# One exponential per attention slot from PSUM, with the sum taken beside it, and earlier strided loads in a fused attention and expert kernel

## The chip, the cores and the metric

The kernel runs on one core of a Trainium2 chip. The metric is the device time of one execution in microseconds, the median of several runs. TensorE (PE) multiplies, VectorE (DVE) and ScalarE (ACT) work elementwise and read PSUM, GpSimd (POOL) only builds masks at the start, and SyncE (SP) issues nearly all the transfers.

## The reference

All is float32. Attention of 2 batches, 8 heads, 576 positions of 64 numbers; the first four heads use a local mask of 32 positions, the last four a strided one (equal position modulo 32). Three products and a sum over four experts follow, on 1152 tokens.

```
scores = where(mask, q @ k.T / 8, -1e9)
scores = scores - max(scores)
attn   = exp(scores);  attn = attn / (sum(attn) + 1e-9)
x      = attn @ v                      # (1152, 512)
x      = ((x @ w1) * (x @ w2)) @ w3 @ w_out
out    = sum over 4 experts of p[:, e] * (relu(x @ e1[e]) @ e2[e])
```

## The kernel before

Every product after attention is made of three, from a high and a low part of each operand (`mm3`). The wide weights w1, w2, w_out and w3 arrive as 64-bit numbers and are turned into float32 and split on ACT and DVE: for each `Chunk` of 1 MB, ACT rounds the low word (L136) and takes the magnitude (L144), DVE clamps, shifts, sets the sign and adds (L147 to L157), ACT makes the high part `w_hi` (L164) and DVE the low part `w_lo` (L174). The generator `work` gives these steps out one at a time; `advance` and `need` drive it. `add` ends a chunk's use of its raw buffer and issues the load of a later one on SP's queue (`load_next`), so a raw load waits there for DVE.

Attention of a batch is cut into six chunks (`Chunk4`), three local ones with six slots of 64 columns and three strided ones with eight slots of 54. A slot is one row of scores for each of the 128 partitions, and all slots of a chunk lie in one bank of PSUM. `attend(b, s)` writes out step s of nine: scores of chunk s+1 on PE, maxima and exponentials of chunk s, sums and normalisation of chunk s-1, transposes of chunk s-2 with their copy out of PSUM by ACT (L375), and values of chunk s-3 with the two halves of the result, x_hi on ACT (L423) and x_lo on DVE (L427). The order of instructions on each engine is the order of the code (a manual schedule), and each engine works its queue in that order. PSUM has three banks for scores and five (`bank`) that products, transposes and values take in turn.

The nine steps of the first batch stand before all products; only dummy matmuls (`keep_warm`) lie between them on PE. The nine steps of the second batch stand between the 32 units of the first product (`run_unit`, two sums of 12 matmuls each, `ab_acc`); each unit ends in a copy on ACT (L462) and a multiplication on DVE (L464). Unit 2i and 2i+1 of a batch need chunk i of w1 and w2, called c0 to c7 below.

The loads of the second batch's strided heads, keys and queries (`load_qk(1, 1)`) and values (`load_v_str(1)`), are issued in the main loop:

```
            run_unit()
            if done == 1:
                load_qk(1, 1)
                load_v_str(1)
```

Of the kernel before, what the change touches and what calls it, by code (L numbers as in the profile page):

```python
# [8 lines left out]
F32 = mybir.dt.float32  # L9
# [4 lines left out]
AF = mybir.ActivationFunctionType  # L14
ALU = mybir.AluOpType
# [3 lines left out]
P = 128  # L19
# [13 lines left out]
SCALE = 1.0 / float(D) ** 0.5  # L33
# [9 lines left out]
def kernel(  # L43
# [13 lines left out]
    nc = tc.nc  # L57
# [8 lines left out]
    small = ctx.enter_context(tc.tile_pool(name="small", bufs=4))  # L66
# [122 lines left out]
    loaded = 0  # L189
# [47 lines left out]
    def advance(n=1):  # L237

        return all([next(worker, False) for _ in range(n)])
# [14 lines left out]
    qk, vals = {}, {}  # L254

    def load_qk(b, g, cut=0):

        tq, tk = (big[b].tile([P, 2, S], F32, tag="big", name=name) for name in ("tq", "tk"))
        pairs = slice(2 * g, 2 * g + 2)
        for c in ([slice(0, cut), slice(cut, S)] if cut else [slice(0, S)]):  # L260
            for t, src, queue in ((tk, kT, nc.sync), (tq, qT, nc.scalar if cut else nc.sync)):
                queue.dma_start(out=t[:, :, c], in_=src[b, pairs, :, c].rearrange("k p n -> p k n"))
        qk[b, g] = (tq, tk)

    def load_v_loc(b, c):

        tv = wp.tile([P, 2, 3, P], F32, tag="w", name="tv_loc")

        def load(dst, rows, t0, n):
            nc.sync.dma_start(out=dst, in_=v_loc[b, :, rows, t0:t0 + n].rearrange("k p t d -> p k t d"))  # L270

        lower, upper, middle = slice(0, 64), slice(64, P), slice(W, 3 * W)
        if c == 0:
            load(tv[lower, :, 0:1], lower, 0, 1)
            load(tv[upper, :, 0:1], middle, 0, 1)
            load(tv[:, :, 1:], slice(0, P), 1, 2)
        elif c == 1:
            load(tv, slice(0, P), 3, 3)
        else:
            load(tv[lower, :, 0:1], lower, 0, 1)  # L280
            load(tv[upper], middle, 3, 3)
            load(tv[lower, :, 1:], middle, 1, 2)
        vals[b, 0, c] = tv

    def load_v_str(b):

        threes = [wp.tile([P, n, P], F32, tag="w", name="tv_str") for n in (8, 4)]
        for tv, t0, n in ((threes[0], 0, 4), (threes[1], 4, 1)):
            for k in range(2):
                nc.sync.dma_start(out=tv[64 * k:64 * k + T3, :2 * n].rearrange("p (h t) d -> p h t d", h=2),  # L290
                                in_=v_str[b, k, :2 * T3, t0:t0 + n].rearrange("(h p) t d -> p h t d", h=2))
        for k in range(2):
            nc.sync.dma_start(out=threes[1][64 * k:64 * k + NB, 2:], in_=v_str[b, k, 2 * T3:2 * T3 + NB, :2])
        vals[b, 1] = threes

    class Chunk4:
# [44 lines left out]

        def maxima(self):
            s = self.slots
            mx = small.tile([P, 8], F32, tag="mx", name="mx")
            nc.vector.tensor_reduce(out=mx[:, :s], in_=self.sc, axis=mybir.AxisListType.X, op=ALU.max)
            self.frame = p_ring[self.index % 4]
            self.p = self.frame[:, :s, :self.nk]
            nc.vector.tensor_tensor(out=self.p, in0=self.sc, in1=self.wide(mx), op=ALU.subtract)

        def wide(self, t):  # L350
            return t[:, :self.slots].unsqueeze(2).to_broadcast([P, self.slots, self.nk])

        def exps(self):
            nc.scalar.activation(self.p, self.p, AF.Exp, scale=SCALE)

        def sums(self):
            s = self.slots
            self.rec = small.tile([P, 8], F32, tag="rec", name="rec")
            rec = self.rec[:, :s]
            nc.vector.tensor_reduce(out=rec, in_=self.p, axis=mybir.AxisListType.X, op=ALU.add)  # L360
            nc.vector.tensor_scalar_add(rec, rec, 1e-9)
            nc.vector.reciprocal(rec, rec)

# [176 lines left out]
    class Weights:  # L540
# [17 lines left out]
        def work(self):  # L558
# [20 lines left out]
            if self.again:  # L579
                for i, u in enumerate(sums):  # L580
                    nc.sync.dma_start(out=u.bitcast(F32), in_=stored[self.at][i])
            else:
                yield from self.split(sums, w)
                for i, u in enumerate(sums):
                    nc.sync.dma_start(out=stored[self.at][i], in_=u.bitcast(F32))
# [121 lines left out]
    with tc.manual_schedule():  # L707
# [17 lines left out]
        load_qk(1, 0)  # L725
        for c in range(3):
            load_v_loc(1, c)
        chunks = [[Chunk4(3 * g + c, b, g, c) for g in range(2) for c in range(3)] for b in range(B)]
        units = [(b, ft, i) for b in range(B) for ft in range(8) for i in range(2)]
        done = 0  # L730
# [3 lines left out]
        def run_unit():  # L734

            nonlocal done, rest
            b, ft, i = units[done]
            need(c_w12[ft])
            block = ab_block(b, ft, i)
            for _ in range(2):  # L740
                next(rest, None)
                next(block)
                advance(1)
            rest = block
            done += 1
            if b == i == 1:
                c_w12[ft].free()

        def attend(b, s):

            nonlocal live
            chunk = chunks[b]
            n = len(chunk)
            if s == 0:
                chunk[0].scores()
            if s + 1 < n:
                chunk[s + 1].scores()
            if s < n:
                chunk[s].maxima()
                chunk[s].exps()  # L760
            if 1 <= s <= n:
                chunk[s - 1].sums()
                chunk[s - 1].normalise()
            if 2 <= s < n + 2:
                chunk[s - 2].transposes()
                chunk[s - 2].evac(nc.scalar.copy)
            if 3 <= s:
                c = chunk[s - 3]
                c.pv()
                c.put()  # L770
                c.put_lo()
                if c.g == 0 or c.c > 0:
                    live -= 1

        for s in range(9):
            attend(0, s)
            keep_warm(8 if s < 8 else 20)
            if s > 3:
                advance(2)
        steps = iter(range(9))  # L780
        while done < 16:
            run_unit()
            if done == 1:
                load_qk(1, 1)
                load_v_str(1)
            if done in (2, 4, 5, 7, 8, 10, 11, 13, 14):
                attend(1, next(steps))
        load_probs()
# [161 lines left out]
```

## Time and profile before

| what | before |
|---|---|
| median of 3 runs | 644.78 us (644.19 to 645.07) |
| the profiled execution | 647.61 us, of which 645.9 us span |
| PE busy | 626.6 us, 97% of the span, 4688 matmuls |
| DVE busy | 454.8 us, 70% |
| ACT busy | 265.0 us, 41% |
| mean granted clock of TensorE | 0.986 of full speed |

The span runs from the first instruction to the last. PE is busy nearly throughout, but its dummy matmuls count as busy too, so the first 35 us can't be read from its share. A granted clock of 1.00 is 2.4 GHz, of 0.50 it is 1.2 GHz.

### The profile page before, as it was taken

To read this page: it belongs to the slowest core of one execution; us is meant where nothing else is said; L and a number is where in the kernel's file an instruction comes from. 1 tells how busy PE (TensorE), PEld (TensorE's weight loads), DVE (VectorE), ACT (ScalarE), POOL (GpSimd) and SP (SyncE) were. 2 spreads that over 40 slices of the span, in tenths; PEclk is the share of its full clock that TensorE was granted. 3 is DMA by queue.
4 is the path that set the end of the run, shared out by engine and by line. 5 is a ranking of instruction groups with operands and counts; after the bars stand their busy time and mean duration, and the time that the engine had idled before them with its cause. 6 is when DMAs were issued, how large, how long until landed. Compare 5 with 4: busy or idle time off the path is not lost.

```text
span 645.9 us, 11412 instructions
## 1 busy us (share of the span) xinstructions
PE 626.6 (97%) x4688; PEld 569.9 (88%) x4688; DVE 454.8 (70%) x825; ACT 265.0 (41%) x455; POOL 4.2 (1%) x19
## 2 busy tenths in 40 slices
PE   9898998999998999999999999999999999999997
PEld 6687888999886999998999889988788989999996
DVE  5887995698875423777787787797776576665843
ACT  3653563566555322433333333344433333333321
POOL 2000000000000000000000000000000000000000
PEclk9799997999998999999999999999999999999999
DMA  8864322144433310234444355434478464656311
GB/s 263 283 235 128 132 71 76 66 142 136 168 132 130 128 54 15 66 131 159 168 156 171 131 196 163 162 131 152 173 248 323 164 246 154 226 183 236 130 66 66
DMA packets 28727, 99.45 MB, mean 154 GB/s; under 512 B 2652, under 2 KB 6740, under 8 KB 26116
## 3 DMA queue, kind: packets, MB, share of 16 engines
q1 hardware_dynamic: 28132, 98.14, 43.5%
q8 instruction: 37, 0.61, 0.4%
q10 hardware_dynamic: 544, 0.59, 0.3%
q14 instruction: 14, 0.11, 0.0%
HBM read 79.58 MB, written 19.14 MB: 153 GB/s over the span
## 4 chain that ended last, share of the span: by engine, by line
PE 71%; DVE 11%; DMA 9%; ACT 5%; issue 3%; SPq 1%; DVEq 0%; ACTq 0%
PE g_acc L247 10%; PE g_acc L248 10%; PE g_acc L249 10%; DMA raw<-in_w3T_dram 4%; PE m_a L247 4%; PE m_a L249 4%; PE m_a L248 4%; PE x_acc L247 3%; PE x_acc L248 3%; PE x_acc L249 3%; PE m_b L249 3%; PE m_c L247 3%; PE m_b L248 3%; PE m_c L248 3%; PE m_c L249 3%
## 5 line engine op out<-in xcount | busy, mean ns | idle before, releaser
L616 ACT ACTIVATE h_hi<-u 128x320 fp32r<-128x320 f32 (+1 forms) x128 | 56.9, 445 | 188.9 <-DVE u L622 188.9
L247 PE MATMUL g_acc<-w_hi,h_hi 128*128 128x512 f32 (+1 forms) x296 | 114.3, 386 | 0.0
L248 PE MATMUL g_acc<-w_lo,h_hi 128*128 128x512 f32 (+1 forms) x296 | 114.2, 386 | 0.0
L249 PE MATMUL g_acc<-w_hi,h_lo 128*128 128x512 f32 (+1 forms) x296 | 113.7, 384 | 0.0
L247 PE MATMUL ab_acc<-x_hi,w_hi 128*128 128x288 f32 x256 | 77.9, 304 | 2.5 <-ACT w_hi L164 1.6
L622 DVE TENSOR_TENSOR u<-m_b,u 128x320 f32<-128x320 f32 (+1 forms) x96 | 40.8, 452 | 53.2 <-PE m_b L249 53.2
L555 DVE TENSOR_TENSOR w_lo<-raw,w_hi 128x768 fp32r<-128x768 f32 x64 | 69.4, 1084 | 12.0 <-ACT w_hi L553 11.9
L249 PE MATMUL ab_acc<-x_hi,w_lo 128*128 128x288 f32 x256 | 76.7, 300 | 0.8 <-DVE w_lo L174 0.8
L248 PE MATMUL ab_acc<-x_lo,w_hi 128*128 128x288 f32 x256 | 76.6, 299 | 0.7 <-DVE x_lo L427 0.7
L249 PEld LDWEIGHTS g_acc<-w_hi,h_lo 128*128 128x128 f32 x296 | 55.6, 188 | 11.6
L247 PEld LDWEIGHTS g_acc<-w_hi,h_hi 128*128 128x128 f32 x296 | 55.8, 188 | 8.0
L248 PEld LDWEIGHTS g_acc<-w_lo,h_hi 128*128 128x128 f32 x296 | 55.7, 188 | 7.6
L618 DVE SCALAR_TENSOR_TENSOR h_lo<-u,h_hi 128x320 fp32r<-128x320 f32 (+1 forms) x128 | 57.6, 450 | 3.5 <-ACT h_hi L616 1.1
L553 ACT CAST w_hi<-raw 128x768 fp32r<-128x768 f32 x64 | 59.9, 936 | 0.0
L247 PEld LDWEIGHTS ab_acc<-x_hi,w_hi 128*128 128x128 f32 x256 | 49.2, 192 | 3.8 <-ACT w_hi L164 1.7
L249 PEld LDWEIGHTS ab_acc<-x_hi,w_lo 128*128 128x128 f32 x256 | 49.1, 192 | 1.2 <-DVE w_lo L174 1.2
L248 PEld LDWEIGHTS ab_acc<-x_lo,w_hi 128*128 128x128 f32 x256 | 49.1, 192 | 0.9 <-DVE x_lo L427 0.9
L248 PE MATMUL m_b<-b_t,s_hi 128*128 128x320 f32 (+1 forms) x128 | 37.9, 296 | 0.0
L622 DVE TENSOR_TENSOR u<-m_a,u 128x320 f32<-128x320 f32 (+1 forms) x64 | 28.8, 450 | 11.6 <-PE m_a L249 11.6
L555 DVE TENSOR_TENSOR s_lo<-raw,s_hi 128x1024 fp32r<-128x1024 f32 x16 | 19.6, 1225 | 23.2 <-ACT s_hi L553 23.2
L136 ACT ACTIVATE raw<-raw 128x1024 int32<-128x1024 uint32 x20 | 23.4, 1168 | 28.4 <-DMA raw<-in_w3T_dram 19.2
L622 DVE TENSOR_TENSOR u<-m_c,u 128x320 f32<-128x320 f32 (+1 forms) x64 | 29.0, 452 | 4.8 <-PE m_c L249 4.2
(151 smaller groups left out, 1392.8 us busy)
## 6 DMA issues: line engine op xcount, KB each, us to landing
raw<-in_e_dram SPq DMA_DIRECT2D x32, 1024.0 KB
raw<-in_w_dram SPq DMA_DIRECT2D x8, 1024.0 KB
raw<-in_w3T_dram SPq DMA_DIRECT2D x8, 1024.0 KB
stored<-s_hi SPq DMA_DIRECT2D x16, 512.0 KB
stored<-s_lo SPq DMA_DIRECT2D x16, 512.0 KB
s_hi<-stored SPq DMA_DIRECT2D x16, 512.0 KB
s_lo<-stored SPq DMA_DIRECT2D x16, 512.0 KB
raw<-in_w_out_dram SPq DMA_DIRECT2D x4, 1024.0 KB
```

The source lines that it names most:

```text
L136: nc.scalar.activation(self.low, self.low.bitcast(U32), AF.Copy, scale=2.0 ** -29)
L247: mm(acc, lh, rh, start=first, stop=False)
L248: mm(acc, lh, rl, start=False, stop=False)
L249: mm(acc, ll, rh, start=False, stop=last)
L553: nc.scalar.copy(dst[0], src)
L555: nc.vector.tensor_tensor(out=dst[1], in0=src, in1=dst[0].bitcast(F32), op=ALU.subtract)
L616: nc.scalar.activation(hi, src, AF.Relu)
L618: nc.vector.scalar_tensor_tensor(out=lo, in0=src, scalar=0.0, in1=hi.bitcast(F32), op0=ALU.max, op1=ALU.subtract)
L622: nc.vector.tensor_tensor(out=out, in0=acc, in1=b, op=ALU.add)
```

## The change

The maximum is multiplied by -SCALE after the reduction (a tiny instruction on DVE), and then each slot has its own ACT instruction that reads the scores from PSUM, takes the slot's maximum as bias and adds its results up into `rec`. The subtraction over the whole chunk (L348) and the sum over the whole chunk (L360) leave DVE. The two loads move: keys and queries go ahead of the main loop, right behind the second batch's local values, and the strided values to the moment when the third raw chunk has been issued.

```diff
         def maxima(self):
             s = self.slots
-            mx = small.tile([P, 8], F32, tag="mx", name="mx")
-            nc.vector.tensor_reduce(out=mx[:, :s], in_=self.sc, axis=mybir.AxisListType.X, op=ALU.max)
+            self.mx = small.tile([P, 8], F32, tag="mx", name="mx")
+            mx = self.mx[:, :s]
+            nc.vector.tensor_reduce(out=mx, in_=self.sc, axis=mybir.AxisListType.X, op=ALU.max)
+            nc.vector.tensor_scalar_mul(mx, mx, -SCALE)
             self.frame = p_ring[self.index % 4]
             self.p = self.frame[:, :s, :self.nk]
-            nc.vector.tensor_tensor(out=self.p, in0=self.sc, in1=self.wide(mx), op=ALU.subtract)
...
         def exps(self):
-            nc.scalar.activation(self.p, self.p, AF.Exp, scale=SCALE)
+            self.rec = small.tile([P, 8], F32, tag="rec", name="rec")
+            for s in range(self.slots):
+                at = slice(s, s + 1)
+                nc.scalar.activation(self.p[:, s], self.sc[:, s], AF.Exp, bias=self.mx[:, at], scale=SCALE,
+                                     accum_out=self.rec[:, at])
 
         def sums(self):
-            s = self.slots
-            self.rec = small.tile([P, 8], F32, tag="rec", name="rec")
-            rec = self.rec[:, :s]
-            nc.vector.tensor_reduce(out=rec, in_=self.p, axis=mybir.AxisListType.X, op=ALU.add)
+            rec = self.rec[:, :self.slots]
             nc.vector.tensor_scalar_add(rec, rec, 1e-9)
             nc.vector.reciprocal(rec, rec)
...
         load_qk(1, 0)
         for c in range(3):
             load_v_loc(1, c)
+        load_qk(1, 1)
...
             if s > 3:
                 advance(2)
+            if loaded == 3 and (1, 1) not in vals:
+                load_v_str(1)
         steps = iter(range(9))
         while done < 16:
             run_unit()
-            if done == 1:
-                load_qk(1, 1)
-                load_v_str(1)
             if done in (2, 4, 5, 7, 8, 10, 11, 13, 14):
```

ACT's queue in steps 4 and 5 of the first batch before (`p_pair` holds the probabilities, `sc` the scores, `mx` the maxima, `tp` the transposes, `o` the values' products, `raw_212` chunk c0's raw words):

```order
L354 ACTIVATE p_pair<-p_pair 128x8x54
L375 COPY pT<-tp 128x384
L423 CAST x_hi<-o 128x2x3x32 x2
L136 ACTIVATE raw_212<-raw_212 128x1024
L354 ACTIVATE p_pair<-p_pair 128x8x54
L375 COPY pT<-tp 128x512
```

The same place in ACT's queue now:

```order
L358 ACTIVATE p_pair,rec<-sc,mx 128x54 x8
L377 COPY pT<-tp 128x384
L425 CAST x_hi<-o 128x2x3x32 x2
L136 ACTIVATE raw_212<-raw_212 128x1024
L358 ACTIVATE p_pair,rec<-sc,mx 128x54 x8
L377 COPY pT<-tp 128x512
```

Nothing changed places; each exponential of a chunk became eight instructions (six for a local chunk) ahead of the same copy and the same x_hi.

DVE's queue in step 4 of the first batch before (maxima of chunk 4, sums and normalisation of chunk 3, x_lo of chunk 1):

```order
L345 TENSOR_REDUCE mx<-sc 128x8
L348 TENSOR_TENSOR p_pair<-sc,mx 128x8x54
L360 TENSOR_REDUCE rec<-p_pair 128x8
L361 TENSOR_SCALAR rec<-rec 128x8
L362 RECIPROCAL rec<-rec 128x8
L365 TENSOR_TENSOR p_pair<-p_pair,rec 128x8x54
L427 TENSOR_TENSOR x_lo<-o,x_hi 128x2x3x32 x2
```

The same step now:

```order
L346 TENSOR_REDUCE mx<-sc 128x8
L347 TENSOR_SCALAR mx<-mx 128x8
L363 TENSOR_SCALAR rec<-rec 128x8
L364 RECIPROCAL rec<-rec 128x8
L367 TENSOR_TENSOR p_pair<-p_pair,rec 128x8x54
L429 TENSOR_TENSOR x_lo<-o,x_hi 128x2x3x32 x2
```

Two long instructions are gone and a tiny one has come; x_lo still stands at the end of the step, ahead of the next step's maxima.

SP's queue of transfers behind the second batch's local values, as a difference (`raw` numbers differ between the builds; the rows taken out are the loads of c2 and c3, the row put in is c2's):

```order
 L270 DMA tv_loc<-in_v_loc_dram 64x2x384
 L270 DMA tv_loc<-in_v_loc_dram 64x2x256
-L132 DMA raw_635<-in_w_dram 128x2048
-L132 DMA raw_733<-in_w_dram 128x2048
 L262 DMA tk<-in_kT_dram 128x2x576
 L262 DMA tq<-in_qT_dram 128x2x576
+L132 DMA raw_669<-in_w_dram 128x2048
 L290 DMA tv_str<-in_v_str_dram 54x2x512 x2
 L290 DMA tv_str<-in_v_str_dram 54x2x128 x2
 L293 DMA tv_str<-in_v_str_dram 18x256 x2
```

Keys and queries now go ahead of c2's load, the strided values between c2's and c3's; before, all of them stood behind c3's load and ahead of c4's.

## Rows read from the trace of the kernel before

**Rows 1.** Busy time by stage: start and end, length, each engine's busy us (instructions), granted clock, DMA
```profile
0.00:34.70 34.70, 30.88 (x605) 23.62 (x606) 25.54 (x57) 15.72 (x34) 4.24 (x19) 0.90 0.86 280
...
60.00:80.00 20.00, 18.86 (x272) 17.48 (x271) 18.68 (x36) 10.88 (x20) 0.00 (x0) 1.00 0.31 107
...
140.00:646.00 506.00, 498.01 (x2984) 453.02 (x2982) 344.92 (x623) 194.00 (x326) 0.00 (x0) 1.00 0.43 153
```

**Rows 2.** Timeline of PE, 34 to 104 us: start, length, instruction, idle time before and its releaser
```profile
36.57 0.40 PE L248 MATMUL ab_acc<-x_lo,w_hi 128*128 128x288 f32 x1 [0.69 <-DVE x_lo L427]
...
58.95 0.52 PE L370 MATMUL tp<-ident,p_pair 128*128 128x128 f32 x3 [2.58 <-DVE p_pair L365]
...
73.48 0.52 PE L370 MATMUL tp<-ident,p_pair 128*128 128x128 f32 x3 [0.78 <-DVE p_pair L365]
...
78.56 0.40 PE L247 MATMUL ab_acc<-x_hi,w_hi 128*128 128x288 f32 x1 [0.37 <-ACT pT L375]
...
87.43 0.63 PE L370 MATMUL tp<-ident,p_pair 128*128 128x128 f32 x4 [0.78 <-DVE p_pair L365]
...
102.01 0.43 PE L247 MATMUL ab_acc<-x_hi,w_hi 128*128 128x288 f32 x1 [1.61 <-ACT w_hi L164]
```

**Rows 3.** Timeline of DVE in the first batch
```profile
17.16 0.61 DVE L348 TENSOR_TENSOR p_pair<-sc,mx 128x432 f32<-128x432 f32 x1
17.68 0.59 DVE L360 TENSOR_REDUCE rec<-p_pair 128x8 f32<-128x432 f32 x1
18.31 0.17 DVE L361 TENSOR_SCALAR rec<-rec 128x8 f32<-128x8 f32 x1
...
23.92 0.61 DVE L427 TENSOR_TENSOR x_lo<-o,x_hi 128x192 fp32r<-128x192 f32 x2
...
36.06 0.85 DVE L427 TENSOR_TENSOR x_lo<-o,x_hi 128x108 fp32r<-128x108 f32 x4
```

**Rows 4.** Timeline of ACT in the first batch
```profile
7.72 0.52 ACT L354 ACTIVATE p_pair<-p_pair 128x384 f32<-128x384 f32 x1 [5.49 <-DVE p_pair L348]
...
14.13 0.57 ACT L354 ACTIVATE p_pair<-p_pair 128x432 f32<-128x432 f32 x1 [1.32 <-DVE p_pair L348]
...
17.80 0.57 ACT L354 ACTIVATE p_pair<-p_pair 128x432 f32<-128x432 f32 x1 [1.62 <-DVE p_pair L348]
18.27 0.46 ACT L375 COPY pT<-tp 128x384 f32<-128x384 f32 x1
18.95 0.54 ACT L423 CAST x_hi<-o 128x192 fp32r<-128x192 f32 x2 [0.22 <-PE o L387]
...
22.44 0.56 ACT L354 ACTIVATE p_pair<-p_pair 128x432 f32<-128x432 f32 x1 [1.54 <-DVE p_pair L348]
...
32.71 0.68 ACT L423 CAST x_hi<-o 128x108 fp32r<-128x108 f32 x4 [0.19 <-PE o L396]
```

**Rows 5.** Groups of ACT by line and shape: count, busy us, mean ns of one
```profile
L354 ACT ACTIVATE p_pair<-p_pair 128x432 f32<-128x432 f32 x6 | 3.4, 566 | 12.4 <-DVE p_pair L348 12.4
...
L423 ACT CAST x_hi<-o 128x36 fp32r<-128x36 f32 x4 | 1.0, 265 | 0.0
L111 ACT ACTIVATE one<-idle 128x1 f32<-128x1 f32 x1 | 0.2, 202 | 0.0
```

**Rows 6.** Timeline of ACT in the second batch
```profile
53.39 1.14 ACT L136 ACTIVATE raw<-raw 128x1024 int32<-128x1024 uint32 x1 [3.60 <-DMA raw<-in_w_dram]
...
72.36 0.46 ACT L375 COPY pT<-tp 128x384 f32<-128x384 f32 x1
...
77.58 0.57 ACT L354 ACTIVATE p_pair<-p_pair 128x432 f32<-128x432 f32 x1 [0.98 <-DVE p_pair L348]
78.05 0.46 ACT L375 COPY pT<-tp 128x384 f32<-128x384 f32 x1
```

**Rows 7.** Timeline of the transfers that SP issues
```profile
38.50 0.43 SPq L262 DMA_DIRECT2D tk<-in_kT_dram  x1
```

**Rows 8.** Busy time by stage, as in the first group, around one stop of PE
```profile
102.00:109.00 7.00, 6.16 (x25) 5.81 (x26) 3.65 (x5) 1.74 (x3) 0.00 (x0) 0.52 0.01 2
```

## The prediction

> **What bounds the kernel now.** I read the stages first. From 140 us on PE works 498.0 of 506 us at full clock [rows 1]: whatever delays PE before that stays in the time, and nothing later gives it back. So the change is judged by how it moves PE's start of the products and PE's stops among the first units. The timeline of PE names these places. The first unit stops for 0.69 us and goes on at 36.57, when the last x_lo of the first batch, from 36.06 on DVE, begins to come in [rows 2, 3]; then there are stops of 2.58, 0.78, 0.37 and 0.78 us at steps of the second batch's attention, and one of 1.61 us for the high part of c7 [rows 2]. Ahead of the first unit PE mostly fills time with dummies. The timelines of DVE and ACT show what leads there: in the first batch DVE runs from one instruction into the next (25.5 of 34.7 us busy, though the first exponential comes only at 7.72), and ACT waits for DVE's subtraction ahead of every exponential, 1.3 to 1.6 us each time in the strided chunks [rows 1, 3, 4]. DVE bounds the first batch, ACT has room there. In the second batch ACT is busy 10.9 of 20 us and DVE 18.7 [rows 1].
>
> **What DVE is spared.** Per strided chunk the subtraction goes (17.16 to 17.68, 0.52 us) and the sum (17.68 to 18.31, 0.63 us); an instruction like L361 comes, 0.20 us with its hand-over [rows 3]. That is 0.95 us less per chunk. It counts only as long as DVE doesn't wait for ACT instead.
>
> **What a slot costs ACT.** The trace shows no exponential with a bias per partition and no sum beside one, so I bound the price p of a slot from its start to the next slot's. From below: four casts of 108 and 36 columns take 0.68 us together; less the length of a short one, 0.265, that is (0.68 - 0.265) / 3 = 0.14 us from start to start [rows 4, 5]. From above: if slot and sum are two instructions that don't overlap, twice the 0.202 us of a one-column ACTIVATE and 54 columns at (566 - 202) / 431 = 0.84 ns, together 0.45 us [rows 5]. Between: a cast of 36 columns from PSUM is 0.265 us [rows 5], so 54 or 64 columns are about 0.28; ACT starts the next instruction 0.10 us before the end (17.80 + 0.57 against 18.27) [rows 4], which leaves 0.18; a second instruction that writes the sum adds 0.202 - 0.10 = 0.10, and a bias read for each partition adds something between nothing and another 0.10. I take p = 0.33 us, an estimate: 1.98 us for six slots and 2.64 for eight, where one instruction took 0.52 and 0.57. The ends 0.14 and 0.45 stay in the range.
>
> A rule of the Trainium skill bears on this price (ScalarE: Activation LUTs, section "What ACT_TABLE_LOAD costs"): an ACTIVATE whose bias is read per partition takes about 280 ns and 0.833 ns per column, and instructions in a row overlap by about 93 ns. That is an estimate of 0.232 us for 54 columns, without the writing of the sum, for which the page has no price. By it alone the sum below would come to -1.5 us instead of +5.0. No row of before shows such an instruction.
>
> **First batch.** Now ACT's queue is the long one, and the order of the rows makes a loop of it: the exponentials of chunk s, the copy of the transposes, x_hi of chunk s-3 on ACT; then x_lo of that chunk on DVE, which stands ahead of the maxima of chunk s+1; then its exponentials. Before, DVE worked on sum and normalisation while ACT did its three; now it has only the normalisation there and waits.
> - The first exponential starts 0.4 us earlier, at 7.3 (no subtraction ahead of it) [rows 3, 4]. Eighteen slots of the three local chunks follow each other, 5.9 us, to 13.2; with one copy, 0.4, chunk 3 starts at 13.6, against 14.13 [rows 4].
> - One turn of the loop: 2.64 for the slots, 0.38 to the end of the copy's issue, 0.54 x_hi, 0.05 hand-over, 0.53 x_lo, 0.60 maxima (a reduction of the same form as the sum), 0.23 scaling and hand-over [rows 3, 4], together 4.97 us; before, the turn took 17.80 - 14.13 = 3.67 [rows 4]. Chunk 4 starts at 18.6 (before 17.80).
> - In the next turn DVE does two steps of weight chunk c0 before the maxima (1.3 us, the difference of the turns of 4.64 and 3.67 and what ACT hid): chunk 5 starts at 24.85 (before 22.44) [rows 4].
> - Its slots end at 27.5; copy and x_hi end at 28.35; x_lo of chunk 2 starts at 28.4, against 23.92 [rows 3]: 4.5 us late. Behind it the sum of chunk 5 is gone, 0.63, and the rest of the queue to the last x_lo is as before. The last x_lo starts 3.85 us late, at 39.9 instead of 36.06, and PE's first unit with it: **+3.9 us**. All 42 slots of the batch lie on this path: 0.42 us for every 0.01 us of p.
>
> **Second batch, the loads.** Before, the second batch's strided keys, queries and values are issued from 38.50 on, ahead of c4's raw words [rows 7]; ACT then idles 3.60 us until these land, at 53.39 [rows 6], and the normalisation for which PE stops 2.58 us at 56.4 is queued on DVE behind c4's clamp, which needs ACT. The loads go to where DMA has room (SP's queue: behind the local values, and behind c2). Then c4's words follow c3's directly and ACT doesn't idle for them: 3.60 us earlier, and ahead of that normalisation DVE is spared a subtraction and a sum, 0.9. Of these 4.5 us the stop needs 2.58; the first chunk's six slots, 1.4 us longer, stand ahead of c4's rounding on ACT and may use up some more, which leaves 0.5 to 1.9. So the stop goes: **-2.6 us**.
>
> **Second batch, the slots.** Per step ACT does its eight slots ahead of the copy of the transposes, and that copy frees the bank that PE takes five allocations later. At 78.56 this is a wait already: exponential 77.58, copy 78.05, its end 78.51, PE goes on at 78.56 [rows 2, 6]. The slots can start 0.4 us earlier than the exponential did, since only the scaling lies ahead, and take 2.64 us for 0.47: the copy ends 1.7 us later. The stop of 0.37 becomes about 2.1. At 73.48 and 87.43 PE waited 0.78 for a normalisation; at 73.48 the copy of the chunk before had ended at 72.82, and 1.7 us later it is last, 1.0 us behind the normalisation [rows 2, 6]; the step at 87.43 has the same order and I give it the same. Together 1.7 + 1.0 + 1.0 = **+3.7 us**, 24 slots, 0.24 us for every 0.01 us of p. For the steps between I add nothing: PE has the products of two units between a copy and the bank's next turn there. The 0.95 us per chunk that DVE is spared hides in this; the stop of 1.61 us at 102.01 stays, since c7's high part stands behind x_hi of the last chunk on ACT as before [rows 2].
>
> **The sum.** 3.9 - 2.6 + 3.7 = +5.0 us. The profiled execution took 647.61 us (span 645.9), 2.8 above the median of 644.78; against that median: **649.8 us**. As a function of p: 5.0 - 66 x (0.33 - p), zero at p = 0.25.
>
> **The rivals.**
> - *The sum is free* (p 0.19 to 0.23: the sum is collected while the slot runs and its writing hides behind the next). For it: short instructions follow each other at 0.14 us [rows 4]; against: a result per slot must be written by something. At 0.21 the time is 5.0 - 7.9 = -2.9, 641.9 us; faster below p = 0.25. At the lower bound 0.14 it is -7.5, 637.3. Chance 0.08; the price 0.23, 643.3 us, another 0.07. The latter is what the skill's page would give.
> - *The slot is dear* (0.40 or more: slot and sum hardly overlap). Everything then hangs on ACT: at 0.40 +9.6, 654.4; at 0.45 +12.9, 657.7. Chance 0.18.
> - *The clock falls once more.* From 102 to 109 us the granted clock is 0.52 after a stop of 1.61 us and sparse work before; half of 6.16 busy us, 3.0, is lost [rows 2, 8]. The new stops of about 2 us could do that again: 652.8. Against it: the stops of 2.58, 0.78 and 0.37 us left it at 1.00 in the stage from 60 to 80 us [rows 1, 2]. Chance 0.11. That the fall at 102 goes away (646.8): 0.06.
> - *The loads don't help*, because the normalisation is late through ACT's slots: +2.6 more, 652.4. Its margin is 0.5 to 1.9 us. Chance 0.07.
> - The forecast: 0.43, with a range of its own from 647 to 653.
>
> Two runs of this kernel tell a difference of about 0.2% (1.3 us) from none. Faster by more: 0.12 (the cheap slots); within: 0.08; slower: 0.80. The range from 644 to 657 leaves out the cheap slots, 0.12, and the dearest, 0.06.
>
> **What the profile after would show.** Right: ACT's slots of the first batch 0.3 us and more apart; DVE waiting for x_hi of ACT ahead of each x_lo; turns of about 5 us between the exponentials of chunks 3, 4 and 5; the last x_lo at about 40 us; no idle ACT at c4's words; PE stopped by ACT's copy `pT` near 80 and 90 us; ACT 20 us busier, DVE 10 us less. Wrong: slots 0.2 us apart would make DVE the bound again and the first unit early. A stop that stays at the first transposes of the second batch would tell against the loads.

## The result, and the profile after

| | before | changed |
|---|---|---|
| median | 644.78 us (643.98 to 645.07, 5 runs) | 648.47 us (646.81 to 650.25, 5 runs) |
| ratio | | 1.0057 (95%: 1.0032 to 1.0083) |
| profiled execution | 647.61 us, span 645.9 | 646.81 us, span 645.0 |
| ACT busy | 265.0 us, 41% | 283.7 us, 44% |
| DVE busy | 454.8 us, 70% | 444.0 us, 69% |

The changed kernel is 3.7 us slower; run again beside another kernel it was at 1.006 (1.0041 to 1.0079), 647.19 us against 643.91. The two profiled executions stand the other way round, since that of before lay 2.8 us above its median and that of the changed kernel is the fastest of its five. So I read the two traces stage by stage, up to the last unit of the first batch's products, and not by their spans.

The groups of ACT's instructions by shape show the new instruction pair: line, engine, operation, count, busy us, mean ns, idle before.

```profile
L358 ACT ACTIVATION_READ_ACCUMULATOR p_pair<-sc,mx 128x1 f32 x84 | 18.1, 216 | 0.0
L358 ACT ACTIVATE p_pair<-sc,mx 128x54 f32<-128x54 f32 x48 | 13.9, 317 | 8.6 <-DVE mx L347 7.3 <-DVE rec L363 1.2
L358 ACT ACTIVATE p_pair<-sc,mx 128x64 f32<-128x64 f32 x36 | 10.8, 324 | 8.4 <-DVE mx L347 8.3
```

Each slot is two instructions, the exponential and a second one that writes the sum. They overlap, so the price is read from starts, in ACT's timeline of the first batch (start, length, instruction, idle before and its releaser):

```profile
12.86 0.31 ACT L358 ACTIVATE p_pair<-sc,mx 128x54 f32<-128x54 f32 x1
13.06 0.19 ACT L358 ACTIVATION_READ_ACCUMULATOR p_pair<-sc,mx 128x1 f32 x1
13.16 0.30 ACT L358 ACTIVATE p_pair<-sc,mx 128x54 f32<-128x54 f32 x1
13.34 0.20 ACT L358 ACTIVATION_READ_ACCUMULATOR p_pair<-sc,mx 128x1 f32 x1
...
15.12 0.51 ACT L377 COPY pT<-tp 128x384 f32<-128x384 f32 x1
15.94 0.54 ACT L425 CAST x_hi<-o 128x192 fp32r<-128x192 f32 x2 [0.30 <-PE o L389]
17.73 0.31 ACT L358 ACTIVATE p_pair<-sc,mx 128x54 f32<-128x54 f32 x1 [1.25 <-DVE rec L363]
...
23.46 0.31 ACT L358 ACTIVATE p_pair<-sc,mx 128x54 f32<-128x54 f32 x1 [1.00 <-DVE mx L347]
```

Eight slots take 12.86 to 15.12, 0.283 us each: 0.19 us from the exponential to the writing of the sum, 0.09 from there to the next exponential. The turns from chunk 3 to 4 and 5 take 4.87 and 5.73 us, where they took 3.67 and 4.64 before [rows 4]. DVE's timeline shows the loop that makes them:

```profile
16.29 0.62 DVE L429 TENSOR_TENSOR x_lo<-o,x_hi 128x192 fp32r<-128x192 f32 x2 [2.56 <-ACT x_hi L425]
...
20.76 0.62 DVE L429 TENSOR_TENSOR x_lo<-o,x_hi 128x192 fp32r<-128x192 f32 x2 [2.18 <-ACT x_hi L425]
...
26.60 0.62 DVE L429 TENSOR_TENSOR x_lo<-o,x_hi 128x192 fp32r<-128x192 f32 x2 [2.22 <-ACT x_hi L425]
...
38.10 0.86 DVE L429 TENSOR_TENSOR x_lo<-o,x_hi 128x108 fp32r<-128x108 f32 x4
```

Before, DVE had waited 0.41 us for ACT ahead of the first of these x_lo, and not at all ahead of the next two:

```profile
15.99 0.62 DVE L427 TENSOR_TENSOR x_lo<-o,x_hi 128x192 fp32r<-128x192 f32 x2 [0.41 <-ACT x_hi L423]
```

Now it waits 2.2 to 2.6 us ahead of each of the three, and the last x_lo starts at 38.10 instead of 36.06. PE's timeline shows what follows from it:

```profile
35.37 4.27 PE L118 MATMUL idle<-idle 128*128 128x256 bf16 x20
39.40 0.38 PE L247 MATMUL ab_acc<-x_hi,w_hi 128*128 128x288 f32 x1
...
45.84 0.34 PE L323 MATMUL sc<-m_loc,i_loc 128*128 128x384 bf16 x1
...
60.02 0.55 PE L372 MATMUL tp<-ident,p_pair 128*128 128x128 f32 x3
...
74.35 0.55 PE L372 MATMUL tp<-ident,p_pair 128*128 128x128 f32 x3 [0.55 <-ACT pT L377]
...
81.44 0.40 PE L247 MATMUL ab_acc<-x_hi,w_hi 128*128 128x288 f32 x1 [2.10 <-ACT pT L377]
...
90.81 0.66 PE L372 MATMUL tp<-ident,p_pair 128*128 128x128 f32 x4 [1.29 <-ACT pT L377]
...
105.58 0.40 PE L247 MATMUL ab_acc<-x_hi,w_hi 128*128 128x288 f32 x1 [1.61 <-ACT w_hi L164]
```

Against [rows 2]: the stop of 2.58 us at the first transposes is gone (60.02, no wait). The other stops of 0.78, 0.37 and 0.78 became 0.55, 2.10 and 1.29 and all wait for ACT's copy. The stop of 1.61 us at c7 stands at 105.58 instead of 102.01, 3.57 us later, near the 3.7 of the medians. PE came to the second batch's scores, the row at 45.84, in the trace of before as follows:

```profile
42.12 0.34 PE L323 MATMUL sc<-m_loc,i_loc 128*128 128x384 bf16 x1
```

That is 3.72 us late; from there to the unit at c7 the changed kernel takes 59.74 us against 59.89, so in between about as much is added as the loads gave back; the experiments size both. And 3.72 is 1.7 more than x_lo is late: here PE was not waiting for x_lo. Its own 20 dummies took 4.27 us, to 39.6, and the first unit behind them found x_lo ready. The busy time by stage gives the reason, the granted clock (the third number from the end):

```profile
0.00:34.70 34.70, 28.28 (x569) 21.06 (x569) 17.96 (x49) 24.10 (x108) 4.26 (x19) 0.87 0.94 291
34.70:42.00 7.30, 7.30 (x62) 6.00 (x58) 6.84 (x12) 4.35 (x8) 0.00 (x0) 0.68 0.64 210
...
60.00:80.00 20.00, 18.72 (x271) 17.23 (x267) 14.13 (x29) 13.77 (x51) 0.00 (x0) 1.00 0.29 96
```

0.68 in the stage in which the first units stand, where before it was 1.00:

```profile
34.70:42.00 7.30, 6.61 (x51) 6.38 (x48) 6.74 (x12) 3.96 (x5) 0.00 (x0) 1.00 0.39 127
```

The clock was at its half level in the first batch before, too, but earlier, and was back when the last dummies came. In the changed kernel it fell near 26 us, where PE had stopped for 2.00 us (for a normalisation) and stopped again for 1.31 us (for a copy of transposes), and came back only after 39 us. First the kernel before, then the changed one:

```profile
24.00:30.00 6.00, 5.94 (x80) 4.32 (x80) 5.86 (x14) 3.46 (x7) 0.00 (x0) 0.50 0.80 220
...
26.00:39.00 13.00, 11.74 (x134) 8.39 (x135) 10.84 (x23) 8.25 (x20) 0.00 (x0) 0.50 0.95 282
```

In the first stage ACT is now the busier engine, 24.1 us to DVE's 18.0, which had been 15.7 and 25.5 [rows 1].

Behind the stop at c7 the two profiled executions differ where the change touches nothing. In both the clock falls behind this stop, but from 102 to 112 us its mean is 0.66 before (first row) and 0.83 in the changed kernel:

```profile
102.00:112.00 10.00, 9.16 (x47) 8.81 (x48) 5.61 (x8) 3.37 (x6) 0.00 (x0) 0.66 0.05 7
...
102.00:112.00 10.00, 7.44 (x69) 6.89 (x68) 5.36 (x11) 3.36 (x9) 0.00 (x0) 0.83 0.14 55
```

So of the 3.57 us only 1.9 are left at the first product that needs w3, whose matmuls start at 164.7 before and at 166.6 in the changed kernel:

```profile
L247 PE MATMUL wc_acc<-w_hi x64: 389/389/632, 164.7 to 211.7; 128*128 128x512 f32 x64
...
L247 PE MATMUL wc_acc<-w_hi x64: 389/389/504, 166.6 to 211.5; 128*128 128x512 f32 x64
```

In the same way near a stop for a weight of w3, before:

```profile
200.00:204.00 4.00, 3.79 (x11) 3.07 (x12) 3.21 (x4) 0.68 (x1) 0.00 (x0) 0.65 0.00 0
```

And of the changed kernel:

```profile
200.00:204.00 4.00, 3.15 (x13) 2.30 (x14) 3.93 (x5) 0.45 (x1) 0.00 (x0) 1.00 0.01 4
```

Both executions stop there for a high part and a low part of w3; in that of before the clock fell behind the stop, in the other it didn't. In the second execution of the changed kernel that was profiled the stage from 195 to 205 us has a clock of 0.87. That such a fall belongs to an execution and not to the kernel is likely by this, and the spans of two single profiles can't decide over 4 us here.

### The profile page after: what moved, and what is told of

Read it like the earlier page. It is cut to its first block, busy times and chain, and to the rows that moved or that the text cites. A ratio compares the mean times of both kernels' runs of the same rounds, so it can differ in the third digit from the quotient of the medians.

```text
span 645.0 us, 11563 instructions
## 1 busy us (share of the span) xinstructions
PE 625.6 (97%) x4688; PEld 568.6 (88%) x4688; DVE 444.0 (69%) x813; ACT 283.7 (44%) x611; POOL 4.3 (1%) x19
## 4 chain that ended last, share of the span: by engine, by line
PE 78%; DVE 8%; ACT 6%; DMA 5%; issue 2%; SPq 1%; DVEq 0%; ACTq 0%
PE g_acc L247 10%; PE g_acc L248 10%; PE g_acc L249 10%; DMA raw<-in_w3T_dram 4%; PE m_a L247 4%; PE m_a L249 4%; PE m_a L248 4%; PE ab_acc L247 3%; PE ab_acc L249 3%; PE ab_acc L248 3%; PE x_acc L249 3%; PE x_acc L247 3%; PE x_acc L248 3%; PE m_b L248 3%; PE m_c L247 3%; PE m_c L248 3%
## 5 line engine op out<-in xcount | busy, mean ns | idle before, releaser
L634 ACT COPY u<-m_a 128x320 f32<-128x320 f32 (+1 forms) x32 | 12.8, 399 | 44.8 <-PE m_a L249 44.8
```

The lines of the kernel that those rows point to most:

```text
L634: nc.scalar.copy(u1, a)
```

## The experiments

All of them were run in five rounds or more beside the kernel before; the ratio is to that kernel, with its 95% interval.

| kernel | median us | ratio | interval |
|---|---|---|---|
| slots, loads as before | 650.13 | 1.0074 | 1.0045 to 1.0104 |
| loads alone | 642.04 | 0.9949 | 0.9929 to 0.9969 |
| loads, slots in the second batch | 645.69 | 1.0011 | 0.9994 to 1.0028 |
| loads, slots in the first batch | 644.08 | 0.9986 | 0.9965 to 1.0006 |
| changed, sum on DVE | 645.69 | 1.0009 | 0.9992 to 1.0025 |
| changed, 8 last dummies | 646.79 | 1.0023 | 1.0006 to 1.0039 |
| changed, slots last in a step | 640.36 | 0.9922 | 0.9902 to 0.9942 |
| loads alone, exponential last | 641.52 | 0.9951 | 0.9931 to 0.9971 |
| changed, again | 647.19 | 1.0060 | 1.0041 to 1.0079 |
| slots last, 8 last dummies | 641.08 | 0.9953 | 0.9937 to 0.9969 |

**The parts of the change.** Four kernels: the slots without the loads, the loads without the slots, and the loads with the slots in one batch only.

```diff
 # slots, loads as before
-        load_qk(1, 1)
...
             run_unit()
+            if done == 1:
+                load_qk(1, 1)
+                load_v_str(1)
```

```diff
 # slots in the second batch only (in the first: self.b == 0)
+            if self.b == 1:
+                nc.vector.tensor_scalar_mul(mx, mx, -SCALE)
+            else:
+                nc.vector.tensor_tensor(out=self.p, in0=self.sc, in1=self.wide(self.mx), op=ALU.subtract)
...
+            if not (self.b == 1):
+                nc.scalar.activation(self.p, self.p, AF.Exp, scale=SCALE)
+                return
...
+            if not (self.b == 1):
+                nc.vector.tensor_reduce(out=rec, in_=self.p, axis=mybir.AxisListType.X, op=ALU.add)
```

> The exponentials per slot of the changed kernel, with the two loads left where they were before. My theory (three terms: the first batch late by 3.7 us, the stop of 2.58 us at the first transposes of the second batch taken away by the loads, 2.4 us more of waits for ACT's copies in the second batch): the stop comes back, in part at least, and the time is 649 to 651 us, 1 to 2.6 above the changed kernel. Rival (the stop went because PE comes later, not because of the loads): as the changed kernel, 648.5, and no stop at these transposes.

> The loads at their new places, the exponentials as before. My theory: only the stop of 2.58 us goes, about 642.2 us. Rival (the loads do nothing by themselves): 644.8, with the stop still there.

> Loads as in the changed kernel; one exponential per slot in the second batch only. My theory: the first batch is on time, the waits for ACT's copies cost 2.4 us: 644.6 us. Rival (in the second batch the slots only swap one wait for another): as with the loads alone.

> Loads as in the changed kernel; one exponential per slot in the first batch only. My theory: PE enters the second batch 3.7 us late and loses nothing there: 646 us. Rival (the first batch's delay is given back in the stream of weights later): within 1 us of the loads alone.

The loads alone gain 0.51% (2.7 us by the medians, as expected); on top of them the slots of the second batch cost 0.62% (1.0011 - 0.9949; 3.7 us by the medians), those of the first 0.37% (2.0 us), together 0.99%, and the changed kernel, which has both, stands 1.08 to 1.11% above the loads. So the three terms are there, and nearly add up. Two of the four times missed what was expected: the first batch's slots cost 2.0 us where 3.7 were expected from the row at 45.84, the second batch's 3.7 where it was 2.4. But two such intervals leave a difference open by some 0.3%, near 2 us. The timelines of PE size the parts more closely, though from one execution of each kernel (in us: the second batch's first scores, PE going on behind the stop at c7, and the time between):

| kernel | scores | behind c7 | between |
|---|---|---|---|
| before | 42.12 | 102.01 | 59.89 |
| loads alone | 42.28 | 99.05 | 56.77 |
| loads, slots in the first batch | 45.58 | 101.84 | 56.26 |
| loads, slots in the second batch | 42.57 | 103.12 | 60.55 |
| changed | 45.84 | 105.58 | 59.74 |
| slots, loads as before | 44.22 | 106.69 | 62.47 |

The loads alone save 3.12 us between the two places: the stop of 2.58 us, and 0.51 of the next one, which falls from 0.78 to 0.27. Against them the slots add 3.78 us there when they stand in the second batch only, and 2.97 in the changed kernel, where PE comes later. The 2.4 us was too low, since it left the 0.51 out. The first batch's slots bring PE to the scores 3.30 us late, and 2.79 us of it are left behind c7, so the rival that this delay is given back altogether (within 1 us of the loads alone) finds no support.

With one exponential per chunk the stop at the first transposes is gone through the loads alone, as PE's timeline of that kernel shows (no wait named):

```profile
56.46 0.55 PE L370 MATMUL tp<-ident,p_pair 128*128 128x128 f32 x3
```

ACT's timeline shows why: it waits 0.40 us for c4's words and rounds them from 50.36 on, where it waited 3.60 and started at 53.39 [rows 6]. In the changed kernel it starts on them at 53.41, late through the slots and without a wait for them.

```profile
50.36 1.16 ACT L136 ACTIVATE raw<-raw 128x1024 int32<-128x1024 uint32 x1 [0.40 <-DMA raw<-in_w_dram]
```

With the slots but the loads at their old places, PE's timeline is this:

```profile
34.99 2.36 PE L118 MATMUL idle<-idle 128*128 128x256 bf16 x20
...
38.67 0.40 PE L248 MATMUL ab_acc<-x_lo,w_hi 128*128 128x288 f32 x1 [0.41 <-DVE x_lo L429]
...
59.17 0.52 PE L372 MATMUL tp<-ident,p_pair 128*128 128x128 f32 x3 [0.71 <-DVE p_pair L367]
...
75.47 0.55 PE L372 MATMUL tp<-ident,p_pair 128*128 128x128 f32 x3 [1.76 <-ACT pT L377]
```

A stop of 0.71 us, not 2.58: the rival has a good part of the truth here. PE comes 2 us later and DVE is spared two instructions ahead of that normalisation. But a later stop is 1.76 us where it is 0.55 in the changed kernel. The dummies in this execution took 2.36 us at full clock, not 4.27, and PE was at the scores 1.6 us earlier than in the changed kernel, yet 1.1 us later behind c7. So beside the slots the loads are worth something from 1.1 us (with this head start) to 2.7 (between the two places); by whole kernels it is 1.0057 to 1.0060 against 1.0074, 1 us, with overlapping intervals.

**Is it ACT's time per slot?** The bias per slot stays, the sum goes back to DVE.

```diff
-                nc.scalar.activation(self.p[:, s], self.sc[:, s], AF.Exp, bias=self.mx[:, at], scale=SCALE,
-                                     accum_out=self.rec[:, at])
+                nc.scalar.activation(self.p[:, s], self.sc[:, s], AF.Exp, bias=self.mx[:, at], scale=SCALE)
...
+            nc.vector.tensor_reduce(out=rec, in_=self.p, axis=mybir.AxisListType.X, op=ALU.add)
```

> The changed kernel with the sum taken back to VectorE (one reduction per chunk); the slots keep the bias from the maximum. Theory (ScalarE's time per slot is what costs): the second instruction per slot, 0.09 us from start to start, falls away 84 times; slots about 0.20 us apart, about 2 us gained in each batch less what the reductions take: 644 to 645.5 us. Rival (the number of instructions in the queue doesn't matter, only that x_lo stands behind them): within 1 us of the changed kernel, 648.5.

1.0009 against 1.0057: 0.5% less, with intervals that don't meet; the median, 645.69, is 0.2 us beyond the theory's figure. ACT's timeline, chunk 3 of the first batch:

```profile
13.33 1.69 ACT L358 ACTIVATE p_pair<-sc,mx 128x54 f32<-128x54 f32 x8 [0.40 <-DVE mx L347]
14.92 0.48 ACT L377 COPY pT<-tp 128x384 f32<-128x384 f32 x1
```

Eight slots take 1.59 us to the start of the copy, 0.20 each, where they took 2.26. The second instruction's 0.09 us per slot is real, and in this order of a step ACT's time per slot sets how much is lost.

**The dummies.**

```diff
-            keep_warm(8 if s < 8 else 20)
+            keep_warm(8)
```

> The changed kernel with 8 dummy matmuls instead of 20 behind the last step of the first batch. In the changed kernel's trace these 20 ran at half clock until 39.6 us, 1.5 us beyond the start of the last x_lo at 38.1. Theory (PE's first unit is held by its own dummies): 1 to 1.5 us faster, 647 to 647.5. Rival (fewer dummies leave the clock low and the first unit runs at half speed): as the changed kernel or up to 1.5 us slower.

1.0023 against 1.0057 and 1.0060: 0.34 to 0.37%, about 2 us, for 12 dummies less, a little more than expected; its interval overlaps the first of the two and not the second. PE's timeline:

```profile
34.81 1.05 PE L118 MATMUL idle<-idle 128*128 128x256 bf16 x8
...
38.78 0.40 PE L248 MATMUL ab_acc<-x_lo,w_hi 128*128 128x288 f32 x1 [1.32 <-DVE x_lo L429]
...
44.32 0.34 PE L323 MATMUL sc<-m_loc,i_loc 128*128 128x384 bf16 x1
```

PE now waits for x_lo, and is at the second batch's scores at 44.32 instead of 45.84. In this execution the clock was back at 1.00 at 34 us, ahead of the eight dummies, and stayed there to 42 us. So it doesn't show what eight dummies do at the half clock, nor what 20 would have cost in it.

How often the 20 dummies fell under the half clock can be counted over the kept traces, one or two executions of each kernel. With the slots in the first batch they took 4.27 and 4.06 us in the changed kernel, 4.03 with slots in the first batch only, 3.92 with the sum on DVE, 3.61 with the slots last in a step, and 2.36 with the loads as before. With one exponential per chunk in the first batch (before, loads alone, slots in the second batch, exponential last) they took 2.36 each time. So the half clock over the dummies came in five of six executions with the slots there and in none of four without; that the slots bring it, by moving PE's stops, is likely and not shown.

**The order in a step.** The same work, with the slots behind the copy and x_hi in ACT's queue, and x_lo last on DVE; and the same order with one exponential per chunk.

```diff
             if s < n:
                 chunk[s].maxima()
-                chunk[s].exps()
-            if 1 <= s <= n:
-                chunk[s - 1].sums()
-                chunk[s - 1].normalise()
             if 2 <= s < n + 2:
                 chunk[s - 2].transposes()
                 chunk[s - 2].evac(nc.scalar.copy)
             if 3 <= s:
                 c = chunk[s - 3]
                 c.pv()
                 c.put()
+            if s < n:
+                chunk[s].exps()
+            if 1 <= s <= n:
+                chunk[s - 1].sums()
+                chunk[s - 1].normalise()
+            if 3 <= s:
                 c.put_lo()
```

> The changed kernel with another order in a step: maxima of chunk s, then the transposes and their copy for chunk s-2, the values and x_hi of chunk s-3, then the slots of chunk s, sums and normalisation of chunk s-1, x_lo of chunk s-3 last. Theory (the cost is that copies and x_hi stand behind the slots on ScalarE): the waits for the copies go and x_lo no longer waits for the slots: 640 to 642.5 us, at or below the loads alone. Rival (ScalarE has too much work in these stages, in any order): 646 to 648.5.

> The loads alone with the same other order in a step, and one exponential per chunk as before. Theory: the copy stood only 0.5 us behind the exponential, so the order changes little: 641.5 to 642.7 us. Rival (the order is worth something by itself): below 641.

With the slots the order is worth 1.35% (0.9922 against 1.0057), 8.7 us; with one exponential nothing (0.9951 against 0.9949). So the cost lay in what stood behind the slots, not in ACT's work as such: ACT is as busy as in the changed kernel, 283.3 us against 283.7. How much of it is the copies' and how much x_hi's and x_lo's, these runs don't part. The waits of PE from 30 to 115 us (waiter, releaser: us in total, times, longest) hold no copy of transposes for products or transposes any more:

```profile
PE ab_acc L247 <- ACT w_hi L164: 1.6, 1, 1.6
PE ab_acc L249 <- DVE w_lo L174: 0.9, 1, 0.9
PE ab_acc L247 <- ACT ab L464: 0.4, 1, 0.4
PE o L398 <- ACT pT L377: 0.2, 1, 0.2
```

And DVE's last x_lo of the first batch starts earlier than in the kernel before:

```profile
35.36 0.85 DVE L429 TENSOR_TENSOR x_lo<-o,x_hi 128x108 fp32r<-128x108 f32 x4
```

This is the fastest kernel of the study, 0.78% ahead of the one before. Against the loads alone and the exponential last, its interval overlaps theirs; that the slots themselves gain in this order isn't shown.

**Once more, and both.**

> The changed kernel again, beside the next one on the same chip, for a steadier number than five runs give. Theory: 648 to 648.7 us, 0.5% above before. Rival (the first figure was high by chance, since the profiled run of it was 646.8): 646 to 647.

> The other order in a step (slots last) together with 8 dummies behind the last step of the first batch. In the trace with 20 dummies these ended at 36.0 us, 0.6 behind the start of the last x_lo at 35.4. Theory: 0.3 to 0.6 us faster than with 20, about 639.9. Rival (fewer dummies let the clock fall in the first units): slower than 640.4 by up to 1.5 us.

The changed kernel's ratio came out the same, 1.0060; its 647.19 us stand against 643.91 for the kernel before in the same set of runs, so the absolute figures moved from one set to another, and the 648 to 648.7 us that were expected were missed while the 0.5% was not. Fewer dummies bring nothing where the slots stand last (0.9953 against 0.9922, with intervals that just overlap), where 0.3 to 0.6 us were expected. In the profiled execution PE was at the second batch's scores 0.57 us earlier (41.59 against 42.16), but 2.07 later behind c7 (99.60 against 97.53). The clock was 1.00 from 34.7 to 42 us, so the rival's fall in the first units isn't what that trace shows; whether fewer dummies cost something there isn't settled.

## Why the prediction was right, and where its sizes were off

Slower was forecast, by 5.0 us, and 3.3 to 3.7 were measured. The path was right, but that the number is so near is in part luck: with the price that a slot turned out to have, the prediction's own formula gives 5.0 - 66 x 0.045 = 2.0 us, and a term that it lacked, the half clock over the dummies (1.7 us), fills the rest.

- **Price of a slot.** 0.33 us was taken, 0.283 and 0.29 measured. The guess that the sum is an instruction of its own, overlapped with its neighbours, is what the trace shows: 0.09 us, and nearly as much (0.283 to 0.20) goes when the sum is taken back to DVE. What is left without it is 0.20 us for 54 columns. The Trainium skill (ScalarE: Activation LUTs, section "What ACT_TABLE_LOAD costs") gives an estimate of 0.232 us for such an instruction; the measured 0.20 is lower, and decides for this kernel.
- **The loop of the first batch.** Right in mechanism and place: x_lo waits for x_hi behind the slots. Chunks 3, 4 and 5 were to start at 13.6, 18.6 and 24.85, and started at 12.86, 17.73 and 23.46, earlier by the cheaper slots. By its own formula, 3.85 - 42 x (0.33 - 0.285) = 2.0, and the last x_lo came 2.04 us late.
- **"and PE's first unit with it".** This step was incomplete. PE's first unit stood behind 20 dummies that ran at half clock, and 1.7 us more went there in the profiled execution of the changed kernel, 1.5 in the second one. The kernel with 12 dummies less was about 2 us faster. The term for this was missing, and the dear price of the slots made up for it in the sum.
- **The loads, -2.6 us.** The stop went, and by themselves the loads gain 2.7 us by the medians, 3.1 up to c7 by the rows, which is the term. But in the changed kernel they are not the only reason: without them the slots left a stop of 0.71, not 2.58, and a later stop of 1.76. Beside the slots this term lies between 1.1 and 2.7 us.
- **The copies behind the slots, +3.7 us.** By the formula for 0.285 us per slot, 3.7 - 24 x 0.045 = 2.6; the trace shows 2.97 against the loads alone. The place worked out in full, the bank that waits for the copy at 78.56, came out at 2.10 as forecast; the two stops to which I gave 1.8 each came out at 0.55 and 1.29. With slots in the second batch only it is 3.78 by the rows and 3.7 by the medians: the same slots cost more there, perhaps because PE comes to them on time.
- **"Nothing later gives it back".** Not so in these executions. Of the 3.57 us at c7, 1.7 went in the next 60 us, through a clock of 0.66 before against 0.83 in the changed kernel behind that stop. Then a stop of PE for a high part of w3 near 199 us was 1.02 us before and 0.48 in the changed kernel (0.84 in its second execution). Both clocks are found with and without the slots: 0.66 over the same ten us with the sum on DVE and, over 98 to 108 us, with the loads alone; 0.83 with the slots in the first batch only and, over 98 to 108, with the exponential last. So this give-back isn't shown to be the change's.
- **The rivals.** The free sum falls (0.09 us per slot), the dear slot too. A fall of the clock did cost time, not at the new stops in the second batch but over the dummies at the end of the first. The fall at 102 didn't go away; it was shorter in both executions of the changed kernel.

What stays open: whether the slots of the first batch cost the 2.0 us of the medians or nearer the 2.8 to 3.3 of the rows, in how many executions the dummies run at half clock, and why the clock stays low for so different a time behind c7.

## What to carry to other kernels

A fused instruction that must be issued once per row group trades one long instruction for many short ones; price it by starts, with the instruction that writes the sum, and then look at what stands behind it in its engine's queue. Here 84 slots cost time because copies and x_hi stood behind them: with these ahead, the same instructions cost nothing measurable. Loads that delay the words an engine waits for are worth moving by themselves, and dummy matmuls that are meant to keep the clock up are work too: 20 of them took 2.36 us at the full clock and 4.27 where it had fallen.

## What the runs showed of the hardware that was not expected

An exponential with a sum shows as ACTIVATE and ACTIVATION_READ_ACCUMULATOR. Within a run of slots the rows of the second kind grow, 0.19 to 0.27 us over the first two chunks, while the starts stay 0.29 us apart, so their lengths, and sums of them, overstate what the slots take:

```profile
7.08 0.19 ACT L358 ACTIVATION_READ_ACCUMULATOR p_pair<-sc,mx 128x1 f32 x1
...
10.07 0.37 ACT L358 ACTIVATE p_pair<-sc,mx 128x64 f32<-128x64 f32 x1
10.27 0.27 ACT L358 ACTIVATION_READ_ACCUMULATOR p_pair<-sc,mx 128x1 f32 x1
```

The same 20 dummies took 2.36 us in one kernel's execution and 4.27 in another's, with the granted clock in that stage at 0.68.
